# Ten of 35 pieces of g turned by VectorE and two transfers through HBM instead of TensorE; a chunk's softmax work put between the two halves of a step

## The chip, the cores and the metric

One core of a Trainium2 chip (trn2) runs the whole program. The metric is device time in microseconds (us) for one execution. TensorE (PE) multiplies, VectorE (DVE) and ScalarE (ACT) do element work and empty PSUM, GpSimd (POOL) helps in the first part, and SyncE (SP) issues every transfer in one queue, in order; 16 DMA engines carry them.

## The reference, cut to what matters

Three stages run one after the other:

```
attn = softmax(q k^T / 8 + decay, causal) v      # 32 heads, 576 positions, 64 wide
x = attn as 2304 tokens x 512
h = x @ w_in                                     # 2304 x 2048
g = h * sigmoid(h)
x = g @ w_out                                    # 2304 x 512
logits = x @ phi                                 # 2304 x 32 slots
d = softmax over tokens of logits;  slot_input = d.T @ x
slot_out = relu(slot_input @ w1[e]) @ w2[e]      # 8 experts, 4 slots each
c = softmax over slots of logits;  out = c @ slot_out
```

## The kernel before, in words

After the attention, which is not touched, the kernel never forms g @ w_out for all tokens. It keeps 2g, folds the half and `phi` into a small matrix WP = w_out @ phi / 2 (`w_prime_a`, `_b`, `_c`), and gets a chunk's logits as WP times the transposed g. Tokens go in 9 chunks of 256 (`c`), the 2048 hidden columns in 4 groups of 512 (`fg`). One pair (c, fg) is a **step**, k = 0 to 35: first the four groups of chunks 0 to 3, then chunk by chunk. The steps from 16 on are chunks 4 to 8.

A step has two halves, t = 0 and 1, of 128 tokens. `h_part` (L554) runs twelve matmuls of 128x512 for a half into one of two PSUM banks; `g_tanh` (L572, ACT) and `g_mul` (L578, DVE, row L583) make 2g of it in SBUF, the page `gt`, and so free the bank. In steps of chunks 4 to 7 all twelve matmuls of a half stand together, and the other work of PE stands at the end of the step:

- `stacked` (L1000): `g_lp` (L610) multiplies turned pieces by WP into the logits `lp`, and adds the chunk's `pp` (`chunk_acc`, L722: softmax weights times g, over all four pieces of a chunk).
- `square` (L1018): `g_tr` (L598) turns a piece of 256 x 512 by eight transposes of 128x128 on PE (`gtp`, row L606), which ACT copies from PSUM to SBUF (`gr`, row L607); `chunk_w` and `chunk_cw` (transposes `etp`, then a chain of small DVE operations); `chunk_soft` (L680: matmul `sl`, then DVE and ACT). `turn_next` takes the next piece, at most two per step; `stacked` of the next step uses them.

There are 36 pieces (c, fg). The last is turned by another function, the other 35 by `g_tr`.

SBUF is handed out in pages of 4 KB a partition from the list FREE, in the order in which they came free. `pump` at the end of a step starts loads of the last stage's weights, 512 KB each (`unit`, L406), while pages are free and up to the number that ROOM gives for the step. They wait in SP's queue for the page's last reader. All work is written by hand in the order in which each engine runs it.

Of the kernel before, what the change touches and what calls it, by code (L numbers as in the profile page):

```python
# [23 lines left out]
OPS = 4  # L24
NPAGES = 25
NW = 8
CAPS = ((0, 12), (5, 6))
LAG = 1
ROOM = ((18, 5), (22, 9), (23, 10), (26, 14), (27, 17), (28, 19), (30, 22), (32, 29), (33, 32), (34, 35), (35, 42), (36, 45))
RING_A, RING_B, RING_T = "014", "235", "b"  # L30


# [1 line left out]
def tile_attention_moe_softmoe(ctx: ExitStack, tc: tile.TileContext, qk, vr, f, wcat, phi, w1, w2, out):  # L34
    nc = tc.nc
# [503 lines left out]
            fn(m)  # L539


    XC, XS, G, GT, GS, GR, LP = {}, {}, {}, {}, {}, {}, {}

    def split_x(c):
        xh, s0 = page([128, 4, CH], "xh", F32R)
# [52 lines left out]
    def g_tr(c, fg):  # L598
        g = GT[c, fg]
        r = w0.tile([128, 4, CH], F32, name="gr", tag="t", bufs=2)  # L600
        for k in range(2):
            tp = bank("t", [128, 2, CH], "gtp")
            for j in range(2):
                for t in range(2):
                    u = 2 * k + j
                    nc.tensor.transpose(tp[:, j, 128 * t:128 * t + 128], g[:, t, 128 * u:128 * u + 128], ident)  # L606
            nc.scalar.activation(r[:, 2 * k:2 * k + 2], tp, AF.Copy)  # L607
        GR[c, fg] = r

    def g_lp(c, fg):  # L610
        r = GR.pop((c, fg))
        if fg == 0:
            LP[c] = ps.tile([128, CH], F32, name="lp", tag=("ava", "b3")[c % 2], bufs=1)
        for u in range(4):
            nc.tensor.matmul(LP[c][32 * u:32 * u + 32], lhsT=sm["WP"][:, 4 * fg + u], rhs=r[:, u],  # L615
                             start=(fg == 0), stop=(fg == 3))

    def w_prime_a(fp):
        wo = WO[fp][0]
# [308 lines left out]
    with tc.manual_schedule():  # L928
        setup()
        for j in range(3):  # L930
            FREE.append((keep, f"ct{j}"))
        for j in range(NW):
            FREE.append((w0, f"w{j}"))
        for i in range(-6, NH + 2):
            if i == -6:
                load(0)
                init_q(1)
                load(1, (1,))
                spread(0)
                spread(1)  # L940
                load(1, (0,))
                init_q(2)
                load(2)
                nc.sync.dma_start(out=cumd, in_=cum.bitcast(F32))
            if i in (0, 3, 5):
                mo["cap"] += 1
            if i == 0:
                pump()
            if i == NH - 6:
                ld.release()  # L950
                mo["r"] = tc.alloc_tile_pool(name="w1p", bufs=1, side="right", reuse_waits="tile")
                FREE.extend((mo["r"], f"r{j}") for j in range(4))
            cv = [(n, i - b) for n, b in enumerate(CONV_AT) if 0 <= i - b < 7]
            att_step(i, cv)
            if i == -2:
                split_lo(0, 1, 0)
                split_lo(0, 1, 1)
            if i == NH + SEL:
                mo.update(last=LAST)
                pump()  # L960
            if i == NH - 1:
                selectors()
                split_x(0)
            elif i == NH:
                FREE.append((nrm, "U2"))
                arena_a()
                split_x(1)
        for p in range(done["r"], NPAIR):
            row_sums(p)
        for p in range(done["n"], NPAIR - 1):  # L970
            norm_b(p)
        for p in range(done["x"], NPAIR - 1):
            norm_x(p)
        for p in range(done["b"], NPAIR - 1):
            norm_c(p)
        att.release()
        mo["p"] = tc.alloc_tile_pool(name="moe", bufs=1, reuse_waits="tile")
        FREE.extend([(mo["p"], f"p{j}") for j in range(NPAGES)] + [(nrm, "U0")])
        arena_b()
        mo.update(cap=CAPS[0][1], spare=SPARE, todo=len(CONV_AT), last=2 * NF)  # L980
        pump()
        steps = [(c, fg) for fg in range(4) for c in range(NJ)] + [(c, fg) for c in range(NJ, NCH) for fg in range(4)]
        rows = [(c + j, fg) for c in (0, 2) for fg in range(4) for j in range(2)]
        rows += [(c, fg) for c in range(4, NCH) for fg in range(4)]
        born, flying, soft, exps, acc = {}, [], [], [], []
        stage = [None, None]

        def turn_next(k):
            if (rows and born.get(rows[0], k) < int(k) and 2 * rows[0][1] + 1 in made
                    and (rows[0][0] < 2 or rows[0][0] - 2 in read) and len(flying) < 2):  # L990
                flying.append(rows.pop(0))
                g_tr(*flying[-1])

        def stacked(k):
            for c, fg in flying:
                g_lp(c, fg)
                if fg == 3:
                    if not soft:
                        chunk_ls(c)
                    soft.append(c)  # L1000
            flying.clear()
            if acc and acc[0][0] < k:
                chunk_acc(acc.pop(0)[1])
            if stage[0] is not None:
                w_prime_b(stage[0])

        def square(k):
            if stage[1] is not None:
                w_prime_c(stage[1])
            stage[1], was = stage[0], len(rows)  # L1010
            stage[0] = mo["wp"].pop(0)[1] if mo["wp"] and mo["wp"][0][0] < k - bool(CQ) else None
            if stage[0] is not None:
                w_prime_a(stage[0])
            else:
                turn_next(k)
            if exps:
                chunk_w(exps[0])
                chunk_cw(exps[0])  # L1018
                acc.append((k, exps.pop(0)))
            turn_next(k)  # L1020
            if soft:
                chunk_soft(soft[0])
                exps.append(soft.pop(0))
                if soft:
                    chunk_ls(soft[0])
            if stage[0] is None:
                turn_next(k)
            if stage[1] is not None and len(rows) < was:
                w_prime_c(stage[1])
                stage[1] = None  # L1030

        conv_ops(OPS)
        for k, (c, fg) in enumerate(steps):
            last = k == len(steps) - 1
            mo["k"] = k
            if k == NJ * 4:
                RINGS.update(h="01", t="254")
            mo["cap"] = [n for at, n in CAPS if k >= at][-1]
            if c == NCH - 1:
                h_part(c, fg, 0, 0, 2)  # L1040
                h_part(c, fg, 1, 0, 2)
                stacked(k)
                square(k)
                h_part(c, fg, 0, 2, 4)
                g_tanh(c, fg, 0)
                g_mul(c, fg, 0)
                h_part(c, fg, 1, 2, 4)
            else:
                h_part(c, fg, 0, 0, 4)
                g_tanh(c, fg, 0)  # L1050
                conv_ops(OPS)
                g_mul(c, fg, 0)
                h_part(c, fg, 1, 0, 4)
            if c in (0, 1) and fg == 0:
                split_x(c + 2)
            elif NJ <= c < NCH - 1 and fg == 1:
                split_x(c + 1)
            elif (c, fg) == (NJ - 1, 3):
                split_x(NJ)
            g_tanh(c, fg, 1, 1 + last)  # L1060
            g_mul(c, fg, 1, 1 + last)
            born[c, fg] = k
            if k == 0:
                norm_b(NPAIR - 1)
                norm_x(NPAIR - 1)
            if k == 3:
                norm_c(NPAIR - 1)
                release((xpool, "x1"), (nrm, "U1"), (nrm, "R"))
            if c < NCH - 1:
                stacked(k)  # L1070
                square(k)
                conv_ops(OPS)
            elif fg != 2:
                stacked(k + 0.5)
                if fg == 1:
                    square(k + 0.5)
            if last:
                ct_page(0)
                ct_page(4)
            mo["umax"] = max([0] + [n for at, n in ROOM if k + 1 >= at])  # L1080
            pump()
        assert not (soft or exps or acc) and not rows[1:] and not mo["wp"], (soft, exps, acc, rows, mo["wp"])
        g_tr_last(*rows.pop(0))
        mo["umax"] = 8 * NE + 8
        pump()
        end()
        tail()
        mo["r"].release()
        xpool.release()
        mo["p"].release()  # L1090
        nrm.release()
        w0.release()
# [42 lines left out]
```

## Time and profile before

| | us |
|---|---|
| three runs: median (lowest, highest) | 561.24 (560.64 to 564.38) |
| the profiled execution: its own time | 558.16 |
| its span, first to last instruction | 556.5 |
| PE busy | 524.7 (94%) |
| DVE, ACT, POOL busy | 328.5, 322.7, 217.8 |
| PE lines in the chain that ended last | 76% |

The span is read as three parts: attention up to about 200 us, the steps from there to about 497 us, and the last stage (the experts and the output) to the end. The change touches the steps 17 to 30, which are 330 to 455 us of this span.

### The profile page before, as it was taken

How to read it: one execution, taken by the hardware profiler on the slowest of the kernel's cores; microseconds unless marked ns; L12 is line 12 of the kernel's file. 1: busy time of each engine (PE TensorE's matmuls, PEld its weight loads, DVE VectorE, ACT ScalarE, POOL GpSimd, SP SyncE). 2: the span in 40 equal slices, each digit the busy share in tenths (PEclk: the TensorE clock that was granted, in tenths of full speed). 3: DMA queues.
4: the chain of work that ended last, by engine and by line, in shares of the span. 5: the costliest groups of instructions: out<-in, count | busy, mean ns of one | idle time of the engine just before them, and what ended most of it. 6: DMA issues, size and time to landing. Idle time of an engine off the chain costs nothing.

```text
span 556.5 us, 11427 instructions
## 1 busy us (share of the span) xinstructions
PE 524.7 (94%) x4243; PEld 380.9 (68%) x4243; DVE 328.5 (59%) x876; ACT 322.7 (58%) x663; POOL 217.8 (39%) x287
## 2 busy tenths in 40 slices
PE   2799999999998999899999999999999999999994
PEld 1577777777776676677776777767767776665562
DVE  5868778877887369999989522332433432335013
ACT  6699899999896666467656544534434433332013
POOL 5788889898897402656456300000000000000000
PEclk9999999999998999999999999999999999999998
DMA  7647675666762457601431511041045027676998
GB/s 222 202 154 226 169 216 168 199 187 188 203 200 51 125 200 256 247 38 61 168 113 57 173 76 39 1 151 39 6 152 185 14 101 276 234 298 261 410 402 316
DMA packets 37067, 94.33 MB, mean 170 GB/s; under 512 B 7540, under 2 KB 13972, under 8 KB 37012
## 3 DMA queue, kind: packets, MB, share of 16 engines
q1 hardware_dynamic: 37012, 93.61, 50.2%
q8 instruction: 33, 0.54, 0.4%
q14 instruction: 22, 0.18, 0.1%
HBM read 83.63 MB, written 9.13 MB: 167 GB/s over the span
## 4 chain that ended last, share of the span: by engine, by line
PE 76%; DVE 10%; ACT 5%; DMA 4%; issue 2%; SPq 1%; POOL 1%; DVEq 0%; ACTq 0%; POOLq 0%
PE h L562 10%; PE h L564 9%; PE h L563 9%; PE av L273 7%; PE gtp L606 6%; PE st L224 5%; PE mx L182 5%; PE st L226 4%; PE lp L615 3%; PE pp L729 3%; PE rs L256 3%; PE so L855 3%; PE h L800 3%; DVE wt L465 2%; DMA KA<-cumd 1%
## 5 line engine op out<-in xcount | busy, mean ns | idle before, releaser
L562 PE MATMUL h<-w,xh 128*128 128x512 f32 x288 | 118.0, 410 | 4.0 <-DVE gt L583 3.8
L564 PE MATMUL h<-w,xh 128*128 128x512 f32 x288 | 113.6, 395 | 0.0
L563 PE MATMUL h<-w,xl 128*128 128x512 f32 x288 | 113.4, 394 | 0.0
L583 DVE SCALAR_TENSOR_TENSOR gt<-gt,h 128x512 f32<-128x512 f32 (+1 forms) x73 | 48.6, 676 | 91.4 <-ACT gt L576 91.4
L576 ACT ACTIVATE gt<-h 128x512 f32<-128x512 f32 (+1 forms) x73 | 42.7, 589 | 77.5 <-PE h L564 67.9
L182 PE MATMUL mx<-KA,QA 127*128 127x256 f32 (+2 forms) x192 | 63.4, 353 | 15.5 <-DMA KA<-cum 9.8
L229 ACT ACTIVATE E<-st 128x256 f32<-128x256 f32 (+2 forms) x192 | 66.1, 386 | 19.5 <-PE st L226 16.0
L775 POOL MEMSET SM<- 128x512 f32 x2 | 1.1, 526 | 186.4 <-ACT gt L576 183.8
L188 DVE CUSTOM_DVE_ANT_0 junk<-mx,mask 128x64 bf16<-128x64 f32 (+3 forms) x128 | 51.2, 420 | 30.8 <-PE mx L182 30.1
L562 PEld LDWEIGHTS h<-w,xh 128*128 128x128 f32 x288 | 54.1, 188 | 19.7 <-DVE gt L583 7.3
L224 PE MATMUL st<-QA,KA 128*128 128x256 f32 (+1 forms) x192 | 61.8, 324 | 1.4 <-ACT E L229 0.9
L564 PEld LDWEIGHTS h<-w,xh 128*128 128x128 f32 x288 | 54.1, 188 | 12.8
L563 PEld LDWEIGHTS h<-w,xl 128*128 128x128 f32 x288 | 54.2, 188 | 11.1
L237 POOL TENSOR_SCALAR_AFFINE_SELECT E<-E 128x128 f32<-128x128 f32 (+1 forms) x160 | 54.6, 366 | 16.8 <-ACT E L229 13.5
L607 ACT ACTIVATE gr<-gtp 128x512 f32<-128x512 f32 x70 | 37.5, 596 | 37.5 <-PE gtp L606 37.5
L226 PE MATMUL st<-QB,KB 128*128 128x256 f32 (+1 forms) x192 | 56.5, 297 | 0.0
L273 PE MATMUL av<-E,VF 128*64 128x320 f32 (+4 forms) x448 | 53.6, 371 | 0.0
L182 PEld LDWEIGHTS mx<-KA,QA 127*128 127x128 f32 x192 | 38.1, 201 | 21.4 <-issue 9.8
L160 POOL TENSOR_TENSOR QB<-q,QB 64x576 fp32r<-64x576 f32 x30 | 42.9, 1432 | 14.5 <-issue 10.7
L224 PEld LDWEIGHTS st<-QA,KA 128*128 128x128 f32 x192 | 35.1, 183 | 12.5 <-ACT w L478 3.5
L158 POOL TENSOR_TENSOR KB<-k,KA 64x576 fp32r<-64x576 f32 x30 | 43.2, 1441 | 0.1
L273 PEld LDWEIGHTS av<-E,VF 128*64 128x64 f32 (+1 forms) x448 | 27.0, 137 | 21.4 <-issue 9.0
(148 smaller groups left out, 871.2 us busy)
## 6 DMA issues: line engine op xcount, KB each, us to landing
unit<-in_w_dram SPq DMA_DIRECT2D x64, 512.0 KB
raw<-in_w_dram SPq DMA_DIRECT2D x32, 512.0 KB
k<-in_qk_dram SPq DMA_DIRECT2D x16, 576.0 KB
q<-in_qk_dram SPq DMA_DIRECT2D x15, 576.0 KB
VF<-in_v_dram SPq DMA_DIRECT2D x16, 320.0 KB
RB<-R SPq DMA_DIRECT2D x64, 72.0 KB
out_dram<-ob SPq DMA_DIRECT2D x18, 256.0 KB
WO<-wt SPq DMA_DIRECT2D x8, 512.0 KB
```

Of the source, the lines that this page charges most:

```text
L158: eng.tensor_tensor(t[0:64, h], src[0:64], KA[p % 3][0:64, h], ALU.subtract)
L182: nc.tensor.matmul(t[:, 0:n], lhsT=qa[0:127, h, 128 * blk:128 * blk + 128], rhs=ka[0:127, h, k0:k0 + n], start=True, stop=True)
L188: nc.vector.tensor_tensor_reduce(out=junk[:, 0:w], in0=t[:, 0:w], in1=mask[:, 448 - w:448], scale=1.0, scalar=Mx[p][:, h] if j == 5 else - ...
L224: nc.tensor.matmul(t[0:m, 0:n], lhsT=ka[:, h, k0:k0 + m], rhs=qa[:, h, 64 + q0:64 + q1], start=True, stop=False)
L226: nc.tensor.matmul(t[0:m, 0:n], lhsT=kb_[:, h, k0:k0 + m], rhs=qb[:, h, q0:q1], start=False, stop=True)
L229: nc.scalar.activation(e[0:m, c0:c0 + n - skip], t[0:m, skip:n], AF.Exp, scale=0.125)
L237: nc.gpsimd.affine_select(out=e, in_=e, pattern=[[1, e.shape[0]]], compare_op=ALU.is_ge, fill=0.0, base=0, channel_multiplier=-1)
L273: nc.tensor.matmul(AVP[p][x][64 * h:64 * h + 64, o0:o0 + n], lhsT=VF[p % 2][0:k, kb, h], rhs=E[2 * p + h][kb][0:k, c:c + n], start=kb == 0 ...
L562: nc.tensor.matmul(o, lhsT=xh[:, d, tok], rhs=w[:, 0], start=(d == 0), stop=False)
L563: nc.tensor.matmul(o, lhsT=xl[:, d, tok], rhs=w[:, 0], start=False, stop=False)
L564: nc.tensor.matmul(o, lhsT=xh[:, d, tok], rhs=w[:, 1], start=False, stop=(d == 3))
L583: nc.vector.scalar_tensor_tensor(g, g, 1.0, h[:, n * j:n * j + n], op0=ALU.add, op1=ALU.mult)
```

## The change

For k = 17 to 29 a step turns fewer pieces on PE. `STEPS = (17, 25, 30)` sets the bounds.

- **Turned far from PE.** `blocks` lets DVE transpose a piece in blocks of 32x32 (one instruction over 128 x 1024) into a page `gb`, and SP writes it to HBM (`far`, 512 KB). In the next step `placed` reads it back by four transfers of 32 partitions (128 KB each, runs of 1 KB), which put the blocks in place (`gr`). `g_lp` multiplies it one step later than a piece turned on PE. Its operand `gr` is then read through a view of eight runs of 32 elements. Ten pieces go this way, at the ends of steps 19, 20 and 22 to 29; their products stand at the ends of steps 21, 22 and 24 to 31.
- **Between the halves.** In the steps 18 to 29 `halfway` turns one piece on PE behind the first half's matmuls (up to step 25), and the softmax work of a chunk (`sl` and what follows it) moves there from the end of the step; in the steps before 32 it always stands there.
- From step 25 on the PSUM rings change: the turned pieces have two banks instead of three, the small softmax products two instead of one.
- ROOM lets some units be loaded some steps earlier: 22 by step 28 instead of 30; from step 32 on it is as before.

```diff
+STEPS = (17, 25, 30)
-ROOM = ((18, 5), (22, 9), (23, 10), (26, 14), (27, 17), (28, 19), (30, 22), (32, 29), ...
+ROOM = ((18, 7), (21, 8), (22, 12), (25, 13), (26, 17), (27, 20), (28, 22), (32, 29), ...
...
+    def blocks(c, fg, own):
+        if own:
+            t, GBS[c, fg] = page([128, 4, CH], "gb")
+        else:
+            t = w0.tile([128, 4, CH], F32, name="gb", tag="t", bufs=2)
+        nc.vector.transpose(t.rearrange("p r (b i) -> p r b i", i=32),
+                            GT[c, fg].rearrange("p t (u r j) -> p r (t u) j", u=4, r=4))
+        FAR[c, fg] = hbm.tile([4, 32, 4, 256], F32, name="far", tag="far", bufs=4)
+        nc.sync.dma_start(out=FAR[c, fg].rearrange("a j r n -> (a j) (r n)"), in_=t.rearrange("p r n -> p (r n)"))
+
+    def placed(c, fg):
+        far = FAR.pop((c, fg))
+        r, GRS[c, fg] = page([128, 4, CH], "gr")
+        for i in range(4):
+            nc.sync.dma_start(out=r[32 * i:32 * i + 32], in_=far[:, :, i].rearrange("a j n -> j a n"))
+        GR[c, fg] = r.rearrange("p a (t u i) -> p u t a i", t=2, u=4)
+        if (c, fg) in GBS:
+            release(GBS.pop((c, fg)))
...
+        def turn_far(k):
+            j = int(ready(0, k))
+            if ready(j, k + 1):
+                c, fg = rows.pop(j)
+                flying.append((k + 1, c, fg))
+                blocks(c, fg, turns[1] > k - 2)
+
+        def turn_soft():
+            if soft:
+                chunk_soft(soft[0])
+                exps.append(soft.pop(0))
+                if soft:
+                    chunk_ls(soft[0])
+
+        def halfway(k):
+            if STEPS[0] < k < STEPS[2]:
+                turns[0] = 1
+                turn_next(k - 0.5)
+            turn_soft()
...
         def stacked(k):
-            for c, fg in flying:
+            flying.sort(key=lambda f: f[0])
+            while flying and flying[0][0] < k:
+                _, c, fg = flying.pop(0)
                 g_lp(c, fg)
...
-            flying.clear()
+            for f in list(FAR):
+                placed(*f)
...
         def square(k):
...
-            if soft:
-                chunk_soft(soft[0])
...
+            if k >= (NCH - 1) * 4:
+                turn_soft()
             if stage[0] is None:
                 turn_next(k)
+            if STEPS[0] <= k < STEPS[2]:
+                turn_far(k)
...
+            if k == STEPS[1]:
+                RINGS.update(t="25", g="b4")
...
                 g_mul(c, fg, 0)
+                halfway(k)
                 h_part(c, fg, 1, 0, 4)
```

How the instructions stand on PE at the end of step 27 before (L562 to L564 are the matmuls of `h_part`, L615 `g_lp`, L729 `pp`, L606 `g_tr`, L685 `sl`):

```order
L562 MATMUL h<-w,xh 128x512
L563 MATMUL h<-w,xl 128x512
L564 MATMUL h<-w,xh 128x512
L615 MATMUL lp<-gr,arena 32x256 x8
L729 MATMUL pp<-gt,arena 32x512 x8
L606 MATMUL gtp<-ident,gt 128x128 x16
L685 MATMUL sl<-small,arena 128x256
L562 MATMUL h<-w,xh 128x512
```

and in the changed kernel at the same place (L635 `g_lp`, L751 `pp`):

```order
L563 MATMUL h<-w,xh 128x512
L564 MATMUL h<-w,xl 128x512
L565 MATMUL h<-w,xh 128x512
L635 MATMUL lp<-gr,arena 32x256 x4
L751 MATMUL pp<-gt,arena 32x512 x8
L563 MATMUL h<-w,xh 128x512
```

The sixteen transposes of two pieces are gone from here, `sl` stands in the middle of an earlier step, and one piece is multiplied instead of two. Over steps 17 to 30 PE's list has 112 transposes where it had 192, and as many of all other rows; they stand in nine more places, the middles of steps 18 to 21, 23 to 26 and 30, of which the last two hold `sl` alone.

On DVE at the ends of steps 26 and 27 in the changed kernel (L584 is `g_mul`, L758 the accumulation of `pp`, L728 to L768 the chain of `chunk_cw`, L616 `blocks`); before, the same rows stood there without L616:

```order
L758 SCALAR_TENSOR_TENSOR arena<-arena,pp 128x512
L728 COPY arena<-etp 128x64
L732 SCALAR_TENSOR_TENSOR arena<-arena 128x1
L739 TENSOR_REDUCE arena<-etp 128x2
L740 TENSOR_TENSOR arena<-etp,arena 128x64
L765 TENSOR_REDUCE arena<-arena 128x2
L766 TENSOR_SCALAR arena<-arena 128x2
L767 RECIPROCAL arena<-arena 128x2
L768 TENSOR_TENSOR arena<-arena 128x64
L616 STREAM_TRANSPOSE gb<-gt 128x1024
L584 SCALAR_TENSOR_TENSOR gt<-gt,h 128x512 x2
L758 SCALAR_TENSOR_TENSOR arena<-arena,pp 128x512
```

The block transpose stands behind the step's accumulation and its small chain, and ahead of the next step's first `g_mul`.

On SP from the end of step 24 to that of step 28 in the changed kernel (L619 writes `far`, L625 reads it into `gr`, L417 loads units); before, the 32 units stood there alone:

```order
L619 DMA far<-gb 128x1024
L417 DMA unit<-in_w_dram 128x1024
L625 DMA gr<-far 32x4x256 x4
L619 DMA far<-gb 128x1024
L417 DMA unit<-in_w_dram 128x1024 x4
L625 DMA gr<-far 32x4x256 x4
L619 DMA far<-gb 128x1024
L417 DMA unit<-in_w_dram 128x1024 x3
L625 DMA gr<-far 32x4x256 x4
L619 DMA far<-gb 128x1024
L417 DMA unit<-in_w_dram 128x1024 x2
L625 DMA gr<-far 32x4x256 x4
```

Between a write and its reads up to four unit loads have been queued.

## Rows read from the trace of the kernel before

**Rows 1.** The page: span; each engine's busy us, share of the span, instructions.

```profile
span 556.5 us, 11427 instructions
PE 524.7 (94%) x4243; PEld 380.9 (68%) x4243; DVE 328.5 (59%) x876; ACT 322.7 (58%) x663; POOL 217.8 (39%) x287
```

**Rows 2.** Windows: us, busy of PE, PEld, DVE, ACT, POOL, granted clock, DMA share, GB/s.

```profile
336.00:456.00 120.00, 120.00 (x802) 86.25 (x801) 41.97 (x116) 52.55 (x118) 0.00 (x0) 1.00 0.23 80
219.00:222.00 3.00, 1.89 (x8) 1.58 (x9) 3.00 (x7) 2.37 (x5) 0.48 (x1) 1.00 0.81 130
225.00:228.00 3.00, 3.00 (x15) 2.41 (x14) 3.00 (x4) 0.02 (x1) 2.92 (x3) 1.00 1.03 411
```

**Rows 3.** The chain that ended last, end of step 25: start, us, what.

```profile
402.11 1.00 PE lp L615 x16
403.11 1.72 PE pp L729 x16
404.83 1.02 PE gtp L606 x8
405.85 0.27 PE etp L705 x2
406.12 1.02 PE gtp L606 x8
407.14 0.58 PE sl L685 x2
```

**Rows 4.** PE's timeline, ends of four `h` groups: start, us, line, op.

```profile
285.45 0.39 PE L564 MATMUL h<-w,xh 128*128 128x512 f32 x1
...
286.47 0.48 PE L562 MATMUL h<-w,xh 128*128 128x512 f32 x1
...
335.95 0.40 PE L564 MATMUL h<-w,xh 128*128 128x512 f32 x1
...
338.60 0.48 PE L562 MATMUL h<-w,xh 128*128 128x512 f32 x1
...
466.70 0.40 PE L564 MATMUL h<-w,xh 128*128 128x512 f32 x1
...
468.44 0.48 PE L562 MATMUL h<-w,xh 128*128 128x512 f32 x1
...
471.08 0.40 PE L564 MATMUL h<-w,xh 128*128 128x512 f32 x1
...
471.98 0.50 PE L562 MATMUL h<-w,xh 128*128 128x512 f32 x1
```

**Rows 5.** DVE's timeline, end of step 25 and in step 27; idle before, releaser.

```profile
402.78 0.69 DVE L583 SCALAR_TENSOR_TENSOR gt<-gt,h 128x512 f32<-128x512 f32 x1 [0.78 <-ACT gt L576]
404.95 0.75 DVE L736 SCALAR_TENSOR_TENSOR arena<-arena,pp 128x512 f32<-128x512 f32 x1 [1.48 <-PE pp L729]
...
407.88 0.22 DVE L746 TENSOR_TENSOR arena<-arena 128x64 f32<-128x64 f32 x1
...
421.78 0.69 DVE L583 SCALAR_TENSOR_TENSOR gt<-gt,h 128x512 f32<-128x512 f32 x1 [2.49 <-ACT gt L576]
```

**Rows 6.** SP's timeline: a small write and its read back; a 512 KB store.

```profile
40.96 0.34 SPq L291 DMA_DIRECT2D R<-sg  x1
...
42.62 0.69 SPq L303 DMA_DIRECT2D RB<-R  x1
...
265.19 0.81 SPq L437 DMA_DIRECT2D raw<-in_w_dram  x2
266.05 0.42 SPq L636 DMA_DIRECT2D WO<-wt  x1
```

**Rows 7.** Who SP's queue waited for: us in total, times, longest.

```profile
SPq L303 <- DMA R<-sg: 15.4, 12, 8.0
SPq L437 <- DMA WO<-wt: 5.8, 1, 5.8
```

More of the change, by code (lines that the diff above doesn't have):

```diff
@@ L26 @@
 NW = 8
+STEPS = (17, 25, 30)
 CAPS = ((0, 12), (5, 6))
 LAG = 1
-ROOM = ((18, 5), (22, 9), (23, 10), (26, 14), (27, 17), (28, 19), (30, 22), (32, 29), (33, 32), (34, 35), (35, 42), (36, 45))
+ROOM = ((18, 7), (21, 8), (22, 12), (25, 13), (26, 17), (27, 20), (28, 22), (32, 29), (33, 32), (34, 35), (35, 42), (36, 45))
 RING_A, RING_B, RING_T = "014", "235", "b"
@@ L539, in conv_ops @@
             fn(m)
-    XC, XS, G, GT, GS, GR, LP = {}, {}, {}, {}, {}, {}, {}
+    XC, XS, G, GT, GS, GR, GRS, GBS, FAR, LP = {}, {}, {}, {}, {}, {}, {}, {}, {}, {}
     def split_x(c):
@@ L616, in g_lp @@
                              start=(fg == 0), stop=(fg == 3))
+        if (c, fg) in GRS:
+            release(GRS.pop((c, fg)))
     def w_prime_a(fp):
@@ L985, in tile_attention_moe_softmoe, with ready @@
         born, flying, soft, exps, acc = {}, [], [], [], []
-        stage = [None, None]
+        stage, turns = [None, None], [2, 0]
+        def ready(j, k):
+            return (len(rows) > j and born.get(rows[j], 99) < k and 2 * rows[j][1] + 1 in made
+                    and (rows[j][0] < 2 or rows[j][0] - 2 in read))
         def turn_next(k):
[L989 to L992, printed above, removed]
+            if turns[0] and ready(0, int(k)):
+                turns[0] -= 1
+                turns[1] = k
+                c, fg = rows.pop(0)
+                flying.append((k, c, fg))
+                g_tr(c, fg)
+        def turn_far(k):
[15 more added lines that the diff above has]
+            turn_soft()
         def stacked(k):
-            for c, fg in flying:
+            flying.sort(key=lambda f: f[0])
+            while flying and flying[0][0] < k:
+                _, c, fg = flying.pop(0)
                 g_lp(c, fg)
@@ L1010, in square @@
             stage[1], was = stage[0], len(rows)
+            turns[0] = 1 if STEPS[0] <= k < STEPS[2] else 2
             stage[0] = mo["wp"].pop(0)[1] if mo["wp"] and mo["wp"][0][0] < k - bool(CQ) else None
@@ L1020, in square @@
             turn_next(k)
-            if soft:
-                chunk_soft(soft[0])
-                exps.append(soft.pop(0))
-                if soft:
-                    chunk_ls(soft[0])
+            if k >= (NCH - 1) * 4:
+                turn_soft()
             if stage[0] is None:
                 turn_next(k)
+            if STEPS[0] <= k < STEPS[2]:
+                turn_far(k)
             if stage[1] is not None and len(rows) < was:
```

## Prediction

> **What bounds the kernel now.** I read the page first: of 556.5 us PE is busy 524.7, and no other engine reaches 60% [rows 1]. Then the busy time by windows: in 336 to 456 us, the steps that change, PE is busy 120.00 of 120.00 us at a granted clock of 1.00 (the 2.4 GHz level), DVE 42, ACT 53, POOL 0, and the DMA engines 0.23 [rows 2]. So here a microsecond less on PE is a microsecond less of span, as long as PE finds no new wait, and the three other resources have room. Third, the chain that ended last: at the end of step 25 it goes through PE alone, 1.02 us for each turned piece, 0.50 for a piece's `lp`, 1.72 for a `pp`, 0.27 for `etp`, 0.58 for `sl` [rows 3]. Last, PE's timeline, since matmuls are pipelined and the chain's price of a group may hold some overlap: the time between the last `h` row ahead of a group and the first behind it.
>
> **What is removed.** PE's list loses 80 transposes, ten pieces. From start to start, a gap with one `lp` is 0.90 us (471.08 to 471.98), with one `lp` and one piece 1.74, with one `lp` and two pieces 2.65 [rows 4]. So a piece is worth 0.84 to 0.91; I take 0.86. The chain's 1.02 is the upper end. Ten pieces: **-8.6 us**, at most -10.2. ACT also loses twenty copies out of PSUM; it was not the bound, so nothing.
>
> **What is moved.** The same `sl`, `etp`, `pp` and `lp` stay on PE, but its `h` stream is now broken in nine more places. Price of a break: eight transposes alone make a gap of 1.02 us (285.45 to 286.47), less the usual 0.23 from one `h` row to the next 0.79, which is less than 0.84, so nothing; an `lp` alone costs 0.90 - 0.23 = 0.67 against 0.50 in company, so 0.17 [rows 3, 4]. I take the middle, 0.085: **+0.8 us**, ends 0 and 1.5. The softmax chain that follows `sl` sits in the half step where DVE stood idle 2.49 us ahead of `g_mul` [rows 5]. That the bank of a half is needed again only one half (12 x 0.23 = 2.8 us) and a gap later covers a `g_mul` that comes a little late. Steps 25 and 26 have `etp` right behind `pp`, without a piece between; two banks for these products keep `etp` from waiting for the accumulation.
>
> **What is added on DVE.** Ten block transposes of 128x1024; no row shows one. A row of 128x512 takes 0.69 [rows 5]: two of them, 1.4 us. This stands ahead of the next step's first `g_mul`, where DVE was idle 2.49 us in step 27, so at 1.4 it is hidden there; what it delays is `far`.
>
> The Trainium skill speaks against this place for a transpose: "VectorE: DVE Perf Modes", section "Rules for kernel authors", leaves a 128x128 transpose to TensorE if PSUM will do as the target, and its section "The three transpose paths" gives VectorE 311 ns for 128x128 in bf16, blocks of 32x32 only. By eight of those (an estimate) the instruction is 2.5 us instead of 1.4. It would then just fill the idle time of [rows 5] and make each trip below 1.1 us longer: a stall between 0 and 3.2, in the middle 1.6, and a sum of -6.2 instead of -7.5. No row of this trace has the instruction, so the trace can't decide between the two.
>
> **What is added on the queues.** SP gets 10 x 0.42 and 40 x 0.69 us of issue [rows 6], 32 us in some 112 us; behind it wait only units, which the last stage needs much later, and by step 32 as many are due as before. The traffic grows by 10 x 1.05 MB in that time, 94 GB/s beside the 80 there are, where 411 is possible [rows 2]. It costs nothing unless **the new wait** does: PE runs in order, so an `lp` whose piece has not come back stops all of PE. I work out the trip for the last five pieces, which have the shortest steps and the most units between, from the end of the `h` rows of the step that issues the block transpose.
>
> - *Landing.* A 4.5 KB write was issued by 41.30 and the read that waits for it began at 42.62: 1.3 us [rows 6]. 512 KB at 411 GB/s add 1.3 [rows 2]. The 512 KB store of 266.05 with two loads ahead of it kept its page 5.8 us [rows 7]; by these prices 1.3 + 3 x 1.3 = 5.2, so the price holds within 0.6.
> - *Reads.* Four issues of 0.69, then 1.6 for the last: 4.4 us after `far` has landed. Or, if later, 1.3 us of data behind the units queued ahead.
> - *Step 25.* DVE's small chain ended at 408.10, 6.0 us after 402.11 [rows 3, 5]; one more `lp` and one piece less make 5.5. Transpose until 6.9, issue 7.3. With four units behind `far` the reads are in at 7.3 + 1.3 + 6 x 1.28 = 16.3. PE reaches the `lp` after two steps: 3.5 + 5.55 + 0.6 + 2.5 + 5.55 = 17.7. Slack 1.4.
> - *Step 26* in the same way: in at 14.0, wanted at 15.8, slack 1.8. *Step 27*: no small chain, accumulation done at 3.1, in at 11.9, wanted at 13.8, slack 1.9. *Steps 28, 29*: transpose starts at 1.4, in at 10.2, wanted at 12.7 and 13.0, slack 2.5 and 2.8.
>
> So nothing is lost at these prices. The reads go to 32 partitions in runs of 1 KB, for which the nearest row is the stretch of the short-run reads, 130 GB/s at 0.81 share, 160 at full share [rows 2]: 3.3 us instead of 1.3. With 2.0 us more, step 25 is short by 0.6 and step 27 by 0.1. I take **+0.3 us**, ends 0 and 0.7. As each stall also delays the pieces behind it, a trip longer by D costs about (D - 1.4) + (D - 1.9) + (D - 2.8), each only where positive: the pieces of 25, 27 and 29, whose times do not overlap.
>
> `lp` now reads its operand in runs of 32 elements. No row shows PE reading that way; ends are 0 and a doubling, 10 x 0.50 = 5.0 us. I take 0: the only rows near it are `lp`'s own.
>
> **The sum.** -8.6 + 0.8 + 0.3 = -7.5. Against the profiled execution, 558.16 in all, that is 550.7. This execution lies 3.1 below the median of the runs, so for the median, 561.24, I forecast **553.7**, 1.3% faster. About 1%, 5.6 us, is what a measurement of this kernel can tell from no change. That each of the ten pieces does leave PE is read from the order of the instructions, so that the change does not do what it says has no chance.
>
> **The rivals.**
>
> *Longer trip, no change.* D between 2.8 and 6.5. For it: ten loads queued ahead held a tiny write back 8.0 us [rows 7], so a transfer waits for what stands in front of it. Against it: at most four units stand there, and they are counted. With D = 4 the stall is 2.6 + 2.1 + 1.2 = 5.9 and the time 559.3. Chance 0.25.
> The Trainium skill, "DMA: Bandwidth & Descriptors", section "Latency and other measured facts", gives an HBM access 0.2 us on average and 2 us at high load; by it two loaded legs would add 3.6 (an estimate), which is this rival. The rows here show the DMA engines far from full.
>
> *Slow operand.* `lp` doubled: -7.5 + 5.0 = -2.5, 558.7, no change. Nothing in the trace speaks for it. Chance 0.07.
>
> *Slower.* The wait for `gr` takes the place of the transposes: from D = 6.5 on the stalls exceed 7.8 + 5.6. The place is each `lp` of a far piece, above all at the ends of steps 27, 29 and 31. At D = 8 the stalls are 6.6 + 6.1 + 5.2 = 17.9, net +10, 571. This needs a trip of 23 us where I count 16. For it speaks only that SP works in order and that `gr` stands behind `far`; against it, the store of [rows 7]. Chance 0.09.
>
> *Full price.* Each piece at the chain's 1.02 and free breaks: -10.2, 551.0. Chance 0.08.
>
> *Forecast*, 551.9 to 555.6: 0.51.
>
> Faster by over 1%: 0.51 + 0.08 = 0.59. Within 1%: 0.25 + 0.07 = 0.32. Slower: 0.09. The range from 551 to 560 leaves out the slower case, the worse end of the longer trip and a little below.
>
> **What would show it.** Right: in the windows of the changed steps PE is still busy throughout, these are 7 to 8 us shorter, the rows of the block transpose are 1.2 to 1.6 us, DVE is still idle ahead of `g_mul`, and the gap around a lone `lp` (steps 28, 29) stays near 0.9. Wrong: idle time of PE or its weight loads ahead of `lp` that ends with `gr<-far`, most at the ends of steps 27, 29, 31 (longer trip); a gap around a lone `lp` well above 0.90 with no wait for `gr` (operand); `h` waiting for `g_mul` (block transpose above 5 us). If the last stage grows, units came later than I hold.

## The result, and the profile of the changed kernel

The changed kernel took **553.26 us** in the median of 4 runs (551.06 to 555.4), the kernel before 560.94 beside it (4 runs): a ratio of 0.987, 95% interval 0.983 to 0.991. Two repeats gave 0.988 (0.984 to 0.992) and 0.9905 (0.987 to 0.994). Forecast was 553.7 with a range of 551 to 560, faster. The number is right, and in part by luck: PE gave back more than was counted, the wait for `gr`, on which the rivals hung, was eight times as long as counted, and the two errors are of nearly the same size.

The page of the changed kernel answers to [rows 1]; the last row is the DMA queue's packets, MB and share of 16 engines' span, which read 37012, 93.61 and 50.2% before:

```profile
span 552.6 us, 11354 instructions
PE 515.8 (93%) x4163; PEld 372.5 (67%) x4163; DVE 342.0 (62%) x886; ACT 312.6 (57%) x643; POOL 217.4 (39%) x287
...
q1 hardware_dynamic: 44212, 104.10, 56.6%
```

PE lost its 80 transposes and 8.9 us of busy time, but the span fell by only 3.9. Single spans are a blunt measure here: the instant at which step 17, the last one that the change leaves alone, ends its `h` rows lies between 327.1 and 332.7 us in the kernels below, whose instructions up to there are the same. So I compare two stretches: **the changed steps**, from the last `h` row of step 17 to the last `h` row of step 31, and **the end**, from there to the end of the span. Where no wait falls into the changed steps they repeat within 0.1 us.

The windows of the changed steps, before and then after (columns as in [rows 2]):

```profile
327.93:460.61 132.68, 132.68 (x873) 96.10 (x872) 45.22 (x125) 56.19 (x126) 0.00 (x0) 1.00 0.21 72
```

```profile
330.14:455.45 125.31, 123.08 (x793) 87.63 (x792) 56.88 (x135) 45.95 (x106) 0.00 (x0) 1.00 0.45 147
```

They are 7.37 us shorter. PE works 9.60 us less and stands idle for 2.23 us, which it did not before. The end went the other way, from 95.89 to 97.15 us. The sum is 7.37 - 1.26 = 6.1; the rest of the 7.7 between the medians is within the scatter of the steps ahead of 17.

The idle 2.23 us stand in one place. PE's timeline at the ends of steps 27 and 29:

```profile
425.41 0.39 PE L565 MATMUL h<-w,xh 128*128 128x512 f32 x1
428.03 0.64 PE L635 MATMUL lp<-gr,arena 128*32 128x256 f32 x8 [2.23 <-DMA gr<-far]
428.46 1.93 PE L751 MATMUL pp<-gt,arena 128*32 128x512 f32 x16
430.32 0.50 PE L563 MATMUL h<-w,xh 128*128 128x512 f32 x1
...
442.12 0.40 PE L565 MATMUL h<-w,xh 128*128 128x512 f32 x1
442.44 0.64 PE L635 MATMUL lp<-gr,arena 128*32 128x256 f32 x8
443.01 0.50 PE L563 MATMUL h<-w,xh 128*128 128x512 f32 x1
```

The `lp` of step 25's piece waits for its reads. The lone `lp` of step 29 makes a gap of 0.89 (442.12 to 443.01), as the 0.90 of [rows 4]. The same piece on SP, which issues its store (L619), the units behind it (L417) and its reads (L625):

```profile
415.14 0.34 SPq L619 DMA_DIRECT2D far<-gb  x1
415.53 2.72 SPq L417 DMA_DIRECT2D unit<-in_w_dram  x4
419.06 2.58 SPq L625 DMA_DIRECT2D gr<-far  x4
```

Step 25's last `h` row ended at T = 407.89 in this execution (407.49 + 0.40, as the 402.11 of the prediction). The store goes out at T+7.3 (7.3 was counted). The first read follows it, once it has landed, at T+11.2, 3.9 us later (2.6 counted), and the last read is issued by T+13.8 (12.7 counted). The data are in only 6.4 us after that (3.6 counted), at T+20.1 instead of T+16.3. PE was there at T+17.9 (17.7 counted). The windows (columns as in [rows 2]) show the DMA engines in that time, of the whole trip first:

```profile
415.00:428.00 13.00, 10.80 (x61) 6.99 (x59) 6.97 (x18) 2.80 (x7) 0.00 (x0) 1.00 0.94 306
...
419.00:421.00 2.00, 2.00 (x15) 1.06 (x8) 1.08 (x4) 0.00 (x0) 0.00 (x0) 1.00 0.92 291
421.00:423.00 2.00, 2.00 (x10) 1.63 (x9) 1.54 (x7) 0.26 (x1) 0.00 (x0) 1.00 1.00 363
423.00:425.00 2.00, 2.00 (x11) 1.60 (x10) 1.38 (x2) 0.60 (x1) 0.00 (x0) 1.00 1.07 288
425.00:427.00 2.00, 0.80 (x4) 0.34 (x2) 0.53 (x1) 0.60 (x1) 0.00 (x0) 1.00 1.09 313
```

They are full, and full they move 288 to 363 GB/s, not the 411 of [rows 2], where nothing but long rows was loaded. The mean share of the whole stretch, 0.45, hides this. Nor are the bytes those of the sum alone: 306 GB/s for 13 us are 4.0 MB, 0.8 more than the store, the four units and the piece that were counted. While the reads were out, SP had already issued the next step's store and units:

```profile
423.71 0.34 SPq L619 DMA_DIRECT2D far<-gb  x1
424.15 2.55 SPq L417 DMA_DIRECT2D unit<-in_w_dram  x3
```

DVE's timeline over the same piece answers to [rows 5], and one row gives all ten block transposes (shortest, median, longest in ns; first and last start):

```profile
411.18 0.75 DVE L758 SCALAR_TENSOR_TENSOR arena<-arena,pp 128x512 f32<-128x512 f32 x1 [1.94 <-PE pp L751]
413.57 0.22 DVE L768 TENSOR_TENSOR arena<-arena 128x64 f32<-128x64 f32 x1
413.87 1.25 DVE L616 STREAM_TRANSPOSE gb<-gt 128x1024 f32<-128x1024 f32 x1
415.04 0.65 DVE L584 SCALAR_TENSOR_TENSOR gt<-gt,h 128x512 f32<-128x512 f32 x1
```

```profile
L616 DVE STREAM_TRANSPOSE gb<-gt x10: 1236/1238/1247, 352.4 to 443.9; 128x1024 f32<-128x1024 f32 x10
```

At this step the transpose fills the idle time ahead of `g_mul`, which follows it without a wait of its own; no `h` row waits for `g_mul` in these steps.

Last, the chain that ended last, near the end (start, us, what), before and after:

```profile
522.13 5.32 PE h L800 x96
```

```profile
518.17 10.59 DMA unit<-in_w_dram
```

Where PE ended this stretch, loads of the last units do in this execution; in the two repeats it is PE again (last experiment).

### The profile page after: what moved, and what is told of

Its sections match the earlier page's. It is cut to its first block, busy times and chain, and to the rows that moved or that the text cites. A ratio compares the mean times of both kernels' runs of the same rounds, so it can differ in the third digit from the quotient of the medians.

```text
span 552.6 us, 11354 instructions
## 1 busy us (share of the span) xinstructions
PE 515.8 (93%) x4163; PEld 372.5 (67%) x4163; DVE 342.0 (62%) x886; ACT 312.6 (57%) x643; POOL 217.4 (39%) x287
## 3 DMA queue, kind: packets, MB, share of 16 engines
q1 hardware_dynamic: 44212, 104.10, 56.6%
## 4 chain that ended last, share of the span: by engine, by line
PE 70%; DMA 12%; DVE 9%; ACT 4%; issue 2%; SPq 1%; POOL 1%; DVEq 0%; ACTq 0%; POOLq 0%
PE h L563 9%; PE h L565 9%; PE h L564 9%; PE av L274 8%; DMA unit<-in_w_dram 6%; PE st L225 6%; PE mx L183 5%; PE gtp L607 4%; PE st L227 4%; PE lp L635 3%; PE rs L257 3%; PE pp L751 3%; DMA R<-sg 1%; DVE wt L466 1%; DMA gr<-far 1%
## 5 line engine op out<-in xcount | busy, mean ns | idle before, releaser
L564 PE MATMUL h<-w,xl 128*128 128x512 f32 x288 | 113.4, 394 | 0.0
L584 DVE SCALAR_TENSOR_TENSOR gt<-gt,h 128x512 f32<-128x512 f32 (+1 forms) x73 | 48.5, 674 | 76.2 <-ACT gt L577 76.2
L183 PE MATMUL mx<-KA,QA 127*128 127x256 f32 (+2 forms) x192 | 63.6, 354 | 16.9 <-DMA KA<-cum 10.2
L564 PEld LDWEIGHTS h<-w,xl 128*128 128x128 f32 x288 | 54.2, 188 | 10.7
L608 ACT ACTIVATE gr<-gtp 128x512 f32<-128x512 f32 x50 | 27.2, 596 | 28.4 <-PE gtp L607 28.4
```

The costliest lines, as they stand in the source:

```text
L183: nc.tensor.matmul(t[:, 0:n], lhsT=qa[0:127, h, 128 * blk:128 * blk + 128], rhs=ka[0:127, h, k0:k0 + n], start=True, stop=True)
L564: nc.tensor.matmul(o, lhsT=xl[:, d, tok], rhs=w[:, 0], start=False, stop=False)
L584: nc.vector.scalar_tensor_tensor(g, g, 1.0, h[:, n * j:n * j + n], op0=ALU.add, op1=ALU.mult)
```

## The experiments

All lengths are those of the changed steps and of the end as defined above. The kernel before, run alone for a second pair, gave 132.62 and 95.84 (132.68 and 95.89 in the first): that is the scatter of a kernel that doesn't wait.

> The kernel before once more, for the scatter of its parts: stretch of steps 18 to 31 132.7 again within 0.3. If the end part from step 31 on is 95.9 again, the 0.7 to 1.6 us that it is longer in the kernels with fewer transposes on PE belong to them; if it is 96.5 or more, they are scatter.

### Whose time is the wait: no transfers at all

```
-        nc.vector.transpose(t..., GT[c, fg]...)
-        FAR[c, fg] = hbm.tile(...)
-        nc.sync.dma_start(out=FAR[c, fg]..., in_=t...)
+        FAR[c, fg] = GT[c, fg]
...
-            nc.sync.dma_start(out=r[32 * i:32 * i + 32], in_=far[:, :, i]...)
+        r = FAR.pop((c, fg))...      # lp reads g itself, in the same runs of 32
```

> Leaves out the block transposes, the writes, the reads and their pages: the ten products read g itself, through the same view in runs of 32. What is left is PE's part of the change. Theory (a piece on PE is worth 1.0 us, a break nothing, and 2.3 us are lost to the wait): stretch 122.5 to 123.3, end part 96 as before, since the pages are free again. Rival (a piece is worth 0.86 and a break 0.085, and the rest of the gain has another source): stretch 124.5 to 125.5. Gaps around a lone lp of 0.9 us say that runs of 32 cost nothing, 1.4 that they double lp.

Its window of the changed steps:

```profile
328.02:450.98 122.96, 122.96 (x794) 87.54 (x792) 45.10 (x125) 45.89 (x106) 0.00 (x0) 1.00 0.19 69
```

No wait, and 122.96 us. So the trip costs the changed kernel 125.31 - 122.96 = 2.35 us, nearly all of it the one wait; without it the kernel took 550.38 (ratio 0.983, 0.979 to 0.987). The end, for which 96 was expected, is 97.52, as long as with the trip: what the end lost is not the transfers' doing. The gap round a lone `lp` is 0.90 here (437.64 to 438.54) and `lp` reads in the same runs of 32, so those runs cost nothing.

### What a break and a piece are worth: the moved softmax alone

```
-            if STEPS[0] <= k < STEPS[2]:
-                turn_far(k)
-ROOM = ((18, 7), (21, 8), (22, 12), (25, 13), ...)
+ROOM = ((18, 5), (22, 9), (23, 10), (26, 14), ...)      # as before
```

> Only the second part of the change: pieces and softmax work between the halves, but all 35 pieces turned on PE, and the loads of units by the numbers of the kernel before. Theory (breaks cost between nothing and 0.1 us, the softmax work saves nothing by being moved): stretch 132.5 to 133.8, ratio to before 0.998 to 1.003. Rival (the move saves the 2 us by which PE's gain was larger than counted): stretch 130 to 131.5, ratio 0.994 to 0.997.

All 80 transposes stay on PE, and its `h` stream is broken in the middle of twelve steps. The window of its changed steps, and one break (PE's timeline, the middle of a step):

```profile
327.11:459.14 132.03, 132.03 (x873) 95.88 (x872) 45.51 (x125) 56.47 (x126) 0.00 (x0) 1.00 0.20 72
```

```profile
389.25 0.39 PE L565 MATMUL h<-w,xh 128*128 128x512 f32 x1
389.48 1.03 PE L607 MATMUL gtp<-ident,gt 128*128 128x128 f32 x8
390.35 0.60 PE L707 MATMUL sl<-small,arena 128*128 128x256 f32 x2
390.60 0.59 PE L563 MATMUL h<-w,xh 128*128 128x512 f32 x1
```

132.03 against 132.65, the mean of the two pairs of before: with twelve breaks the steps are 0.6 us **shorter**, between the two expectations. The rows show that no break costs a start of its own: piece and `sl` together fill a gap of 1.35 (389.25 to 390.60), against 1.02 for the eight transposes alone, so the `sl` adds 0.33 there. At a step's end in the kernel before it adds 0.47: the gap at the end of step 24, which holds an `sl`, is 3.94 (392.22 to 396.16), and that of step 28, the same without it, 3.47 (434.19 to 437.66). The whole kernel took 558.37 (0.9975, 0.995 to 1.000): no difference.

Against the kernel without transfers, which differs in the ten pieces, the numbers of its loads and, as those pieces are gone, has nine breaks instead of twelve, 132.03 - 122.96 = 9.07, so 0.91 a piece. With the same numbers of loads (last experiment) it is 9.04.

### Is it the order in SP's queue: units ahead of the store

```
             if STEPS[0] <= k < STEPS[2]:
+                mo["umax"] = max([0] + [n for at, n in ROOM if k + 1 >= at])
+                pump()
                 turn_far(k)
```

> The loads of units are put into SP's queue ahead of the step's block transpose and its write, not behind them; nothing else moves. Theory (the four units between the write of step 25 and its reads make the trip 20 us long): the wait at the end of step 27 disappears, the stretch of steps 18 to 31 is 122.5 to 123.5, the ratio to the changed kernel 0.995 to 0.997. Rival (the reads themselves, 32 partitions in runs of 1 KB, are slow): at least 1 us of wait is left there, stretch 124 or more.

The window of its changed steps, and PE's timeline at the ends of steps 28 and 29:

```profile
330.38:458.38 128.00, 124.69 (x793) 88.65 (x792) 56.91 (x135) 45.91 (x106) 0.00 (x0) 0.99 0.43 144
```

```profile
433.72 0.40 PE L565 MATMUL h<-w,xh 128*128 128x512 f32 x1
435.89 0.64 PE L635 MATMUL lp<-gr,arena 128*32 128x256 f32 x8 [1.77 <-DMA gr<-far]
...
438.62 0.63 PE L563 MATMUL h<-w,xh 128*128 128x512 f32 x1
439.05 0.63 PE L564 MATMUL h<-w,xl 128*128 128x512 f32 x1
...
445.38 0.64 PE L635 MATMUL lp<-gr,arena 128*32 128x256 f32 x8 [1.54 <-DMA gr<-far]
```

The wait of step 27 is gone, and in its place are two, of 1.77 and 1.54 us, for the pieces of steps 26 and 27: units issued first hold up the store instead of the reads. The longest wait of SP for a `far` to land grew from 3.7 to 7.0 us. So half of the expectation holds (the wait of step 27 goes, but the steps are not 122.5 to 123.5 us): another order does not take the wait away, it moves it. The whole kernel took 556.33 (0.993, 0.990 to 0.995). The changed steps came to 128.00 us, 2.7 more than in the changed kernel and 5.04 more than without transfers, though the two waits sum to 3.31. The other 1.7 us are PE's own: after the 1.77 us the `h` rows are 0.43 us apart (438.62 to 439.05) instead of 0.23, in the middle of their stream. The windows show a lower granted clock there (the column ahead of the DMA share):

```profile
436.00:438.00 2.00, 2.00 (x13) 1.30 (x11) 0.75 (x1) 0.00 (x0) 0.00 (x0) 0.79 0.80 182
438.00:440.00 2.00, 2.00 (x6) 1.51 (x6) 0.00 (x0) 0.00 (x0) 0.00 (x0) 0.50 0.92 377
```

### Is it the bytes: the same order, fewer units beside the pieces

```
-ROOM = (..., (25, 13), (26, 17), (27, 20), (28, 22), (32, 29), ...)
+ROOM = (..., (25, 13), (26, 14), (27, 16), (28, 18), (31, 22), (32, 29), ...)
```

> Of the nine units that were loaded at the ends of steps 25 to 27 in the changed kernel (4, 3, 2), four go to the end of step 30, behind the last read of a piece; 1, 2 and 2 stay. Theory (in steps 25 to 28 the DMA engines are near full, so what stands between a write and its reads, or ahead of it, decides the trip): the wait at the end of step 27 is gone and none takes its place, stretch of steps 18 to 31 122.8 to 123.5 us, two less than the changed kernel; the end part is at most 1 us longer. Rival (the trip itself is too long for two steps, as in the kernel with the units ahead): at least 1.5 us of waits of lp for gr in steps 27 to 31, stretch 124.5 or more.

Behind the stores of steps 25, 26 and 27 stand 1, 2 and 2 units instead of 4, 3 and 2; the other four follow at the end of step 30. The windows of its changed steps and of the 13 us from just before step 25's store, SP's timeline of that trip, and PE's at the end of step 27:

```profile
327.67:450.66 122.99, 122.99 (x793) 87.54 (x792) 56.91 (x135) 45.91 (x106) 0.00 (x0) 1.00 0.45 142
...
412.50:425.50 13.00, 13.00 (x85) 7.67 (x83) 6.94 (x18) 2.80 (x7) 0.00 (x0) 1.00 0.65 208
```

```profile
412.61 0.34 SPq L619 DMA_DIRECT2D far<-gb  x1
413.00 0.65 SPq L417 DMA_DIRECT2D unit<-in_w_dram  x1
417.18 1.74 SPq L625 DMA_DIRECT2D gr<-far  x4
```

```profile
422.93 0.39 PE L565 MATMUL h<-w,xh 128*128 128x512 f32 x1
423.25 0.64 PE L635 MATMUL lp<-gr,arena 128*32 128x256 f32 x8
```

No wait for any of the ten pieces: 122.99 us, the length without transfers, with all transfers in it. The store is no quicker: from its issue to the first read 4.6 us pass, 3.9 in the changed kernel. The reads are: they are in within 4.3 us of the last issue (418.92 to 423.25), where the changed kernel took 6.4, and the engines' share in the 13 us is 0.65 instead of 0.94. So it is the bytes in flight beside the trip, queued ahead of the reads or behind them, that made it late.

The repeat:

> The version with the units spread once more beside the changed kernel: no wait of lp for gr, stretch 122.8 to 123.3. If the 2.4 us show in the time of whole runs, its ratio to before is 0.983 to 0.986; if the scatter of the parts that were not changed covers them, its interval overlaps that of the changed kernel.

The changed steps are 123.00 us, the end 96.39 (96.44 in the first), and the whole kernel 551.63 after 552.78; the ratios to before are 0.983 (0.979 to 0.988) and 0.988 (0.983 to 0.992). The changed kernel beside it:

> The changed kernel beside it: stretch 125.3 to 125.6 with the wait at the end of step 27, ratio to before 0.985 to 0.990.

> The changed kernel once more, for comparison in the same rounds. The time from the last h row of step 17 to the last of step 31 was 132.7 us before and 125.3 in the changed kernel; from there to the end of the span 95.9 and 97.2. If this is the change and not scatter, the first is 125 to 126 again, with one wait of lp for gr of 2 to 2.5 us at the end of step 27, and the second 96.5 to 97.5. If the wait is chance, it is missing or stands at another step. Ratio to before 0.983 to 0.991.

In these two the changed steps are 126.64 and 125.52 us, with waits at the end of step 27 of 3.06 and 2.31 (and 0.44 at the end of step 29 in the former, which is 1.0 us longer than was expected of it). So this version beats both kernels in the changed steps, by 2.3 to 3.6 us the one and by 9.7 the other. For whole runs its two ratios to before overlap those of the changed kernel; run beside each other, though, six runs of it (549.17 to 552.89) have a median of 551.63 and eight of the changed kernel (552.23 to 557.88) one of 555.18, 3.5 us apart, which agrees with the 3.6 us between their changed steps.

### Is it the short runs of the reads

```
-        for i in range(4):
-            nc.sync.dma_start(out=r[32 * i:32 * i + 32], in_=far[:, :, i].rearrange("a j n -> j a n"))
+        nc.sync.dma_start(out=r.rearrange("p a n -> p (a n)"), in_=far.rearrange("a j r n -> (a j) (r n)"))
```

> Leaves out the placing of the blocks: far is read back by one plain transfer to 128 partitions in rows of 4 KB instead of four to 32 partitions in runs of 1 KB. Theory (bytes ahead in the DMA engines set the trip): the wait at step 27 falls by the issue time saved, about 1.4 us, to some 0.9, stretch 123.8 to 124.5. Rival (the short runs are slow): it is gone and the engine time of all transfers falls by 10 us or more in sum over the 16 engines' mean share.

One read of 4 KB rows in place of four of 1 KB runs. PE's row at the end of step 27:

```profile
425.83 0.64 PE L634 MATMUL lp<-gr,arena 128*32 128x256 f32 x8 [0.39 <-DMA gr<-far]
```

The wait fell from 2.23 to 0.39, by 1.84 (one run: 552.04 us); 0.9 was expected. Most of that is issue: counted from step 17's last `h` row, the one read is issued by 90.12 (419.57 + 0.33 - 329.78) and the last of four by 91.50 (421.64 - 330.14), 1.38 later. The other 0.46 is less than the waits of the changed kernel differ by among themselves (2.23 to 3.06), so a cost of the short runs is not shown. Nor does the queue show one: it is busy for 309 us of 16 engines (56.1% of 550.3), and for 309 to 315 in the three profiles of the changed kernel, with the same 104.10 MB. The rival's 10 us are not there.

### Is it the transpose: twice as long

```
         nc.vector.transpose(t..., GT[c, fg]...)
+        nc.vector.transpose(t..., GT[c, fg]...)
```

> Each block transpose is issued twice, so DVE does 10 x 1.24 us more. Theory (DVE has the room, and a longer transpose only makes each trip longer): the wait at step 27 grows from 2.3 to 3.4 or 3.7 us, no row of h waits for g_mul, stretch 126.3 to 127.3 as long as the clock holds. Rival (DVE is near its bound): h waits for g_mul in several steps, stretch 129 or more.

PE's timeline at the end of step 27, and a window of the step behind it:

```profile
427.48 0.64 PE L637 MATMUL lp<-gr,arena 128*32 128x256 f32 x8 [3.71 <-DMA gr<-far]
427.91 3.00 PE L753 MATMUL pp<-gt,arena 128*32 128x512 f32 x16
```

```profile
430.00:432.00 2.00, 2.00 (x10) 0.97 (x4) 1.05 (x2) 0.00 (x0) 0.00 (x0) 0.50 1.10 242
```

With a second instruction of 1.25 us the wait for the latest piece is 3.71, as expected, which is 1.5 more than in the first profile of the changed kernel and 0.65 more than in its longest; a wait of 0.25 stands at the end of step 29, and no `h` row waits for `g_mul`. So DVE has the room; how much of the longer wait is the instruction's, one run does not show. The steps are 128.71 us, more than the 126.3 to 127.3 that were expected as long as the clock holds, and 3.4 more than in the changed kernel (one run: 555.33 us in all). The waits make 1.7 of that; the other 1.7 are again a granted clock of 0.50 behind the wait, with a `pp` of 3.00 instead of 1.93.

### The end: is it the loads' numbers

```
     (no transfers, as above, and)
-ROOM = ((18, 7), (21, 8), (22, 12), (25, 13), ...)
+ROOM = ((18, 5), (22, 9), (23, 10), (26, 14), ...)
```

> The kernel without block transposes and transfers again, but with the numbers of the kernel before for the loads of units. Stretch 123.0 again. The part from step 31 to the end was 95.8 to 96.1 us in the three runs with the old numbers and 96.4 to 97.5 in seven with the new. If the numbers (which unit is loaded when and into which page) make the difference, it is 95.8 to 96.2 here; if it comes with the shorter steps, 96.5 to 97.5.

The changed steps are 122.99, the end 97.14 (one run: 554.53 us). So neither the transfers nor the numbers of units make the end longer. It is 96.06 where all transposes stay on PE (the moved softmax alone) and 96.4 to 97.5 in each kernel whose changed steps are shorter. The loads of the last units, to which the chain of the changed kernel points, are not the common cause: they stand in the chain of the moved softmax alone too, whose end is short, and not in those of the two repeats and of this kernel. The chain's last row of an engine, in the kernel before and in the first repeat:

```profile
549.38 0.60 ACT ob L845
```

```profile
543.60 0.60 ACT ob L867
```

and SP's wait for the output to land, in the same two (us in total, times, longest):

```profile
SPq L1128 <- DMA out_dram<-ob: 2.2, 1, 2.2
```

```profile
SPq L1182 <- DMA out_dram<-ob: 2.8, 1, 2.8
```

Counted from step 31's last `h` row, ACT ends at 89.37 before and at 89.35 in the repeat (549.98 - 460.61, 544.20 - 454.85). What is longer stands behind it, in part in that wait: it is 2.2 us in all three traces with every transpose on PE, 2.5 to 3.0 in most of the others. In the two longest ends (97.15 and 97.52) ACT ends 0.5 and 0.9 us later as well, and there the unit loads are in the chain. Why the output lands later I have no run for, and the cause stays open.

## Why the prediction came out right, term by term

- **Pieces, -8.6 (0.86 each, 0.84 to 0.91):** right, at the upper end. 9.07 us, 0.91 each.
- **Breaks, +0.8 (ends 0 and 1.5):** wrong sign, outside its ends. -0.6 with twelve breaks. I priced a break by an `lp` alone, 0.67 against 0.50, and carried half of that over to pieces and `sl`; the rows of the broken stream show that these cost no more in the middle than at the end of a step. With the pieces, PE's part of the change is 132.65 - 122.96 = 9.7 us, where the sum has 7.8; that is nearer to the 10.2 of the rival *full price*.
- **The wait, +0.3 (ends 0 and 0.7):** the place was right (step 25's piece, the end of step 27), the size wrong: 2.35, with 2.6 and 3.7 in the repeats. The step that failed is "in at 16.3, slack 1.4": the piece was in at 20.1. The landing took 3.9 instead of 2.6, and the reads were in 6.4 behind their last issue where the sum leaves 3.6 (16.3 - 12.7). I took 411 GB/s for six transfers of 0.52 MB; with store and short reads among them the full engines moved 314 in the mean (of the rows from 419 to 427). By that, 3.15 MB are 10.0 us instead of 7.7, an estimate that explains 2.3 of the 3.8 by which the piece was later than counted. The sum also has no term for what is issued behind the reads while they are out, the next step's store and units; no run takes these away alone. That the engines are "far from full" was read from the mean of the stage.
- **The rival "longer trip"** thus had the right length, D = 4 (3.8 measured), but a price of 5.9 of which two fifths came due. It let the pieces of 27 and 29 be as late as that of 25. They were not: two units and none stand behind their stores, where four stand behind that of 25. Only in one repeat did the piece of 27 come late, by 0.44. My sum held because D was too small and the price for D too high.
- **The block transpose, 1.4 (1.2 to 1.6):** right, 1.24 us, hidden. The Trainium skill's "VectorE: DVE Perf Modes", section "The three transpose paths", with 311 ns for a 128x128 tile, made it 2.5 by eight of those (an estimate). The measurement decides: a transpose of 128x1024 in f32 takes half of that. The Trainium skill's rule in the same page ("Rules for kernel authors"), to leave such a transpose to TensorE, does not hold here, where TensorE is the bound and gains 0.91 us for each.
- **`lp` on runs of 32, 0 (ends 0 and 5.0):** right, gaps of 0.89 and 0.90 against 0.90.
- **The last stage** I held unchanged. It grew by 0.5 to 1.7 us in every kernel without the transposes. My sign for this, units that came later, explains it in two profiles at most: with the old numbers it grew as well, and in the repeats all of it lies behind the last work of an engine.

Together: -9.07 - 0.6 + 2.35 + 1.3 = -6.0, against -6.1 between the two profiles from step 17 on. The forecast was -7.5. The breaks were 1.4 and the pieces 0.5 better than counted, the wait 2.05 and the end 1.3 worse: 1.5 us too hopeful in all. That 7 to 8 us came out in the changed steps is luck in the terms: PE was not busy throughout, as the prediction asked of itself, and its larger gain paid for the wait.

## What to carry to other kernels

A trip through HBM that PE waits for is timed by the bytes that are in flight beside it, and not by its own alone; the DMA share to look at is that of the trip's own 13 us (0.94 here), not of the stage (0.45). Spread the loads that can wait before you reorder them: moving four units out of the way, three of them from behind one store, removed the wait, putting the units ahead of the stores made two. And price a wait with room for the clock: two of the six long ones here cost about one and a half times to twice their length.

## What the hardware showed that I had not expected

- **The granted clock after a wait.** Behind waits of 1.77 and 3.71 us of PE it fell to 0.50, the lower of its two levels (1.2 GHz), for some 3 us; behind waits of 1.54, 2.23, 2.31 and 3.06 it stayed at 1.00, so the length of the wait alone does not decide.
- **Full DMA engines at 288 to 363 GB/s** with a store, loads and reads in 1 KB runs together, against 411 with long rows alone. The ten trips cost 30 to 37 us of the 16 engines' time (309 to 315 us in the three profiles of the changed kernel, 278 and 279 in the two of the kernel before), 3.0 to 3.7 us for each 1.05 MB.
- **A break in this stream of matmuls cost nothing** where eight transposes or an `sl` stand in it (-0.6 us for twelve).
